# Sparse attention and gated FFN on one core: the last 128 rows of output in two column parts, 384 and 128

## The chip, the cores and the metric

One core of a Trainium2 chip runs the whole program. The metric is the device time in microseconds (us); the runs shown of the kernel before have a median of 295.41 us (five runs, 294.80 to 295.67). Apart from these, one execution was taken with the hardware profiler; all views below come from it.

## The reference

```python
# q, k, v: [4, 8, 768, 64] float32; chunk = 32, top_k = 6
ub   = sum(max(q * k_min[chunk], q * k_max[chunk]))      # bound of each query for each chunk of 32 keys
sel  = the 6 chunks of highest ub, causal chunks only
attn = softmax(where(sel & causal, q @ k.T / 8, -1e9))
x    = (attn @ v) as rows of 8 heads * 64                # [3072, 512]
gate = sigmoid(x @ w_gate); val = x @ w_val              # [3072, 1536]
out  = (gate * val) @ w_out                              # [3072, 512] float32
```

## The kernel before, in words

The 3072 rows of tokens are worked off in eight units `u0` to `u7` of 384 rows, that is three blocks of 128. For each unit there is an attention part (choice of chunks, scores, exponentials, values) and then `ffn(u, ...)` (L1131), the gated FFN of its 384 rows. The attention of a unit is woven into the FFN of the unit before it; the FFN of `u7` stands at the end with nothing beside it.

In `ffn`, twelve steps `fb` each multiply the transposed rows `xT_u` by a slice of 128 columns of `w_gate` into `g_u` and of `w_val` into `v_u` (four matmuls of 384 columns each, L1146). ScalarE (ACT) takes the tanh of `g_u` (L1154), VectorE (DVE) makes `hg_u` = (tanh + 1) * `v_u` (L1158). After that comes the output product, L1162 to L1181, three times, once for each block `tb` of 128 rows: three planned operations `o0`, `o1`, `o2` of four matmuls each add twelve products of `hg_u` (as the weights that are loaded into the array, 128x128) and `wo16` (512 columns) into one PSUM bank `o_u` (L1168); ACT or DVE scales it by 0.5 into the SBUF buffer `osb` (L1177, L1178); SyncE (SP) issues one DMA that stores 128 rows of 512 floats, 2048 bytes a row, to `out` (L1180).

```python
for tb in range(3):
    o = ps(f"o_{u.name}_{tb}", "ff", [128, 512])
...
    plan.add(f"out_{u.name}_{tb}", {SP: (350, 350)}, lambda e, r=r, osb=osb: nc.sync.dma_start(
        out[r:r + 128, :], at(osb)), reads=[osb], writes=[], prio=next_(EV) - 50, dma=(690, 2048))
```

The order of the work is planned before anything is emitted. Every operation is entered with `plan.add`: the engines that may do it with a cost for each, what it reads and writes, a priority. `Plan.walk` (L110) then places one operation after another on the engine on which it can start first, with PSUM banks (eight, of which category "ff" may hold four) and SBUF slots (two for `osb`) given out as they come free. Priorities are moved by a table of nudges (L304), and each DMA has an entry in a table of landing times, `LANDS`, by name. What comes out is one list, and each engine gets its instructions in the order of that list. The stores of outputs and the loads of q, k and v are issued by SP on one DMA queue; the weights are loaded by GpSimd (POOL). After its last store SP waits, one semaphore after the other, until all DMAs have landed, and then the engines meet at a barrier that ends the program (L1303).

Of the kernel before, what the change touches and what calls it, by code (L numbers as in the profile page):

```python
# [10 lines left out]
AF = mybir.ActivationFunctionType  # L11
# [5 lines left out]
PE, ACT, DVE, POOL, SP = "PE", "ACT", "DVE", "POOL", "SP"  # L17
# [486 lines left out]
q10_3:136270 q11_3:139900 v_2_5:126790 v_3_0:140810 v_3_1:141960 v_3_2:143110 out_u5_0:226380 out_u5_1:229010  # L504
out_u5_2:232390 v_3_3:144260 v_3_4:145410 v_3_5:146560 out_u6_0:260540 out_u6_1:263290 out_u6_2:266500
out_u7_0:284690 out_u7_1:287280 out_u7_2:290410
"""


def act(n, psum=True, parts=128):  # L510
    took = (170 if psum else 195) + n / 1.2
    return (took - 105 if parts == 128 else took + 10, took)


def dve(n, rate=1, parts=128):
    took = 158 + n / 0.96 / rate
    return (took - 80 if parts == 128 else took + 10, took)
# [7 lines left out]
def pe(busy, lag=170):  # L525
    return {PE: (busy, busy + lag)}
# [3 lines left out]
def kernel(  # L530
# [10 lines left out]
    nc = tc.nc  # L541
# [9 lines left out]
    NFB = D_FF // 128  # L551
    scale = 1.0 / (D ** 0.5)
# [5 lines left out]
    plan = Plan(  # L558
# [3 lines left out]
    )  # L562

    def at(b):
        if b.tile is None:
            b.tile = (banks if b.kind == "ps" else rot).tile(b.shape, b.dtype, tag=f"{b.kind}{b.slot}", name=b.name)
        return b.tile

    def ps(name, cat, shape, dtype=F32):
        return Buf("ps", name, shape, dtype, cat)  # L570
# [9 lines left out]
    def lone(name, shape, dtype=F16):  # L580
        return keep.tile(shape, dtype, tag=name, name=name)
# [10 lines left out]
    wo16 = lone("wo16", [128, NFB, 512])  # L592
# [6 lines left out]
    class Unit:  # L599
# [59 lines left out]
    units = [  # L659
        Unit(0, [], [(0, 0), (1, 1), (2, 2)]),  # L660
        Unit(1, [(0, 1), (0, 2), (0, 3)]),
        Unit(2, [(0, 4), (0, 5)], [(3, 2)]),
        Unit(3, [(1, 1), (1, 2), (1, 3)]),
        Unit(4, [(1, 4), (1, 5), (2, 1)]),
        Unit(5, [(2, 2), (2, 3), (2, 4)]),
        Unit(6, [(2, 5), (3, 1), (3, 2)]),
        Unit(7, [(3, 3), (3, 4), (3, 5)]),
    ]

    def rank(base, span, count):  # L670

        n = [0]

        def next_(ahead=0.0):
            n[0] += 1
            return base + span * min(1.0, (n[0] - 1) / count) - ahead

        return next_
# [12 lines left out]
    for i in range(2):  # L691
        const(f"kcr{i}", {DVE: (270, 280)}, lambda e, i=i: nc.vector.memset(kcr[i], 0.0),
              writes=[("kcr", i, jb, p, m) for jb in range(NBLK) for p in range(NP) for m in range(2)], prio=-8 if i == 0 else -1)
    for e_ in range(2):
        const(f"hq{e_}", {DVE: (150, 160)}, lambda e, e_=e_: nc.vector.memset(hq[1][e_][MASK[e_], :, 0:64], 0.0),
              writes=[("hqm", 1, e_, p, "zero") for p in range(NP)])
    for i in range(2):
        const(f"ap{i}", {DVE: (400, 410)}, lambda e, i=i: nc.vector.memset(ap[i], 0.0),
              writes=[("ap", i, 0), ("ap", i, 1)], prio=-0.5 + i)
        const(f"v1{i}", {POOL: (260, 300)}, lambda e, i=i: nc.gpsimd.memset(v16[i][:, :, :, D:D + 1], 1.0),  # L700
              writes=[("v16", i, jb) for jb in range(NBLK)], prio=-9 + 6 * i)
        for e_ in range(2):
            for o in range(2):
# [3 lines left out]
                      reads=[epat], writes=[("hkp", i, e_, p) for p in range(o, NP, 2)], prio=0.3 + 0.2 * i, port=True)  # L707
    const("ident16", {DVE: (150, 230)}, lambda e: nc.vector.tensor_copy(ident16, ident32),
          reads=["ident32"], writes=["ident16"], prio=-1.0)
# [421 lines left out]
    def ffn(u, base, span):  # L1131
        next_ = rank(base, span, NFB * 4 + 3 * 5)
        EV = 0.1
        hgs = []
        xt = [(u.xt, c) for c in range(4) if u.m] + [(u.xt, c, x) for c in range(4) for _, x in u.first]
        for fb in range(NFB):
            g = ps(f"g_{u.name}_{fb}", "ff", [128, T])
            w_ = ps(f"v_{u.name}_{fb}", "ff", [128, T])
            gate = Buf("gate", f"gate_{u.name}_{fb}", [128, T], F16)
            hg = Buf("hg", f"hg_{u.name}_{fb}", [128, T], F16)  # L1140
            hgs.append(hg)

            def product(t, w16, fb=fb):
                def emit(e):
                    for c in range(4):
                        nc.tensor.matmul(at(t), w16[:, c, 128 * fb:128 * fb + 128], at(u.xt)[:, c, :],  # L1146
                                         start=(c == 0), stop=(c == 3))
                return emit

            op = plan.add(f"g_{u.name}_{fb}", pe(650), product(g, wg16), reads=xt + [("wg", fb // 4)], writes=[g, "ffn"],  # L1150
                          prio=next_())
            plan.hold(op, gate)
            plan.hold(op, hg)
            plan.add(f"tanh_{u.name}_{fb}", {ACT: act(T)}, lambda e, g=g, gate=gate: nc.scalar.activation(  # L1154
                at(gate), at(g), AF.Tanh, scale=0.5), reads=[g], writes=[gate], prio=next_(EV))
            plan.add(f"v_{u.name}_{fb}", pe(650), product(w_, wv16), reads=xt + [("wv", fb // 4)], writes=[w_, "ffn"],
                     prio=next_())
            plan.add(f"hg_{u.name}_{fb}", {DVE: dve(T)}, lambda e, w_=w_, gate=gate, hg=hg: nc.vector.scalar_tensor_tensor(  # L1158
                at(hg), at(gate), 1.0, at(w_), ALU.add, ALU.mult), reads=[gate, w_], writes=[hg], prio=next_(EV))
        rows = {x: S * b + 128 * ib for x, (b, ib) in enumerate(u.blocks)}  # L1160
        rows.update({x: S * b for b, x in u.first})
        for tb in range(3):  # L1162
            o = ps(f"o_{u.name}_{tb}", "ff", [128, 512])
            osb = Buf("osb", f"osb_{u.name}_{tb}", [128, 512])
            for j in range(3):
                def project(e, o=o, tb=tb, j=j):
                    for fc in range(4 * j, 4 * j + 4):
                        nc.tensor.matmul(at(o), at(hgs[fc])[:, 128 * tb:128 * tb + 128], wo16[:, fc, :],  # L1168
                                         start=(fc == 0), stop=(fc == NFB - 1))

                op = plan.add(f"o{j}_{u.name}_{tb}", pe(4 * 215.6), project,
                              reads=hgs[4 * j:4 * j + 4] + [("wo", j)], writes=[o, "ffn"],
                              prio=next_())
                if j == 0:
                    plan.hold(op, osb)
            plan.add(f"osb_{u.name}_{tb}", {ACT: act(512), DVE: dve(512)}, lambda e, o=o, osb=osb: (
                nc.scalar.activation(at(osb), at(o), AF.Copy, scale=0.5) if e == ACT  # L1177
                else nc.vector.tensor_scalar_mul(at(osb), at(o), 0.5)), reads=[o], writes=[osb], prio=next_(EV))  # L1178
            r = rows[tb]
            plan.add(f"out_{u.name}_{tb}", {SP: (350, 350)}, lambda e, r=r, osb=osb: nc.sync.dma_start(  # L1180
                out[r:r + 128, :], at(osb)), reads=[osb], writes=[], prio=next_(EV) - 50, dma=(690, 2048))  # L1181


    for u in units:
# [25 lines left out]
    for ib in range(1, 4):  # L1210
        cast_v(0, ib, 0.5)
    ffn(units[0], 1.0, 0.95)

    load_wide(units[2], 0.1)
# [4 lines left out]
    for ib in range(4, 6):  # L1219
        cast_v(0, ib, 1.5)  # L1220
    attend(units[1], 1.0)
    ffn(units[1], 2.0, 0.95)

    def values_of(b, blocks, load, base):
# [11 lines left out]
    attend(units[2], 2.0)  # L1236
    first(units[2], 3, 2, raw_f[3], 2.0)
    ffn(units[2], 3.0, 0.95)

    values_of(1, range(4, 6), 2.1, 3.2)  # L1240
# [67 lines left out]
```

The softmax here doesn't subtract the row's maximum and nothing guards it: scores larger than these inputs give would overflow.

## Time and profile before

| what | before |
|---|---|
| median of the five runs shown | 295.41 us |
| the profiled execution's own time | 295.41 us |
| its span in the profile | 293.7 us |
| mean granted TensorE clock | 0.988 |
| PE busy (matmuls) | 277.6 us, 95% |
| ACT busy | 195.5 us, 67% |
| DVE busy | 188.5 us, 64% |
| stores of output, L1180 | 24 of 256 KB |
| start of the last block's scaling on ACT, L1177 | 289.88 us |
| issue of the last store on SP, L1180 | 290.50 us |
| end of the span | 293.7 us |

Times within the profile count from the span's start. The execution's own time is longer than the span by 1.7 us, which lie outside of what the profile shows. PE is TensorE's matmuls, PEld its weight loads, which lie beside matmuls; SPq is the queue of SyncE, which issues DMAs. In a chain of waits each line is a piece of the work that ended last: its start, its length, engine, tile and line.

### The profile page before, as it was taken

What the parts mean: (1) busy time and instruction counts of PE and PEld (TensorE: products, weight loads), DVE (VectorE), ACT (ScalarE), POOL (GpSimd) and SP (SyncE); (2) the same over time, 40 slices, a digit from 0 to 9 for tenths busy, and PEclk for the clock granted to TensorE, in tenths of its full rate; (3) what the DMA queues carried; (4) which work ended last, traced back from release to release, by engine and by line L of the source; (5) the groups of instructions that cost most, each with busy time, mean ns of one, the idle gap of its engine ahead of it and who ended that gap; (6) DMA issues with size and microseconds to landing.
All of it is one profiled execution on the core that took longest, in us unless ns stands there. A gap on an engine that the chain in (4) does not pass through costs nothing.

```text
span 293.7 us, 6954 instructions
## 1 busy us (share of the span) xinstructions
PE 277.6 (95%) x2656; PEld 176.3 (60%) x2656; DVE 188.5 (64%) x560; ACT 195.5 (67%) x398; POOL 91.6 (31%) x162
## 2 busy tenths in 40 slices
PE   2769998999989999999999999999999999999994
PEld 1544655767664666556666667676565556655651
DVE  8285883996999289999899899654134124432420
ACT  7674747977984879558889898886563467323321
POOL 5672314933652336013426854213000011000000
PEclk9977999999999999999999999999999999999999
DMA  7999999999977999299996300001100110011002
GB/s 158 219 250 217 197 197 241 220 146 165 150 135 93 203 187 204 47 215 161 140 218 134 105 3 3 0 2 39 71 2 1 54 56 0 2 38 71 0 16 93
DMA packets 123234, 32.69 MB, mean 111 GB/s; under 512 B 111425, under 2 KB 120129, under 8 KB 123201
## 3 DMA queue, kind: packets, MB, share of 16 engines
q1 hardware_dynamic: 118448, 27.53, 52.3%
q0 software_dynamic: 4752, 4.72, 9.5%
q8 instruction: 21, 0.34, 0.6%
q14 instruction: 13, 0.10, 0.1%
HBM read 30.67 MB, written 6.29 MB: 126 GB/s over the span
## 4 chain that ended last, share of the span: by engine, by line
PE 73%; DMA 12%; DVE 7%; SPq 3%; POOL 2%; issue 1%; ACT 0%; DVEq 0%; ACTq 0%
PE o_u L1168 20%; PE g_u L1146 16%; PE v_u L1146 16%; PE sc_u L1063 10%; DMA wo<-in_moe_w_out_dram 9%; PE pv_u L1096 6%; SPq L742 2%; PE ube_u L1002 2%; DMA kq_u<-in_k_dram 2%; DMA k<-in_k_dram 2%; PE xps_u L1123 2%; DVE kcr L787 1%; DVE kt L953 1%; DVE kx L787 1%; DVE qf_u L969 1%
## 5 line engine op out<-in xcount | busy, mean ns | idle before, releaser
L1074 ACT ACTIVATE att_u<-sc_u 128x512 f16<-128x512 f32 (+3 forms) x184 | 88.1, 550 | 14.3 <-PE sc_u L1063 13.4
L1158 DVE SCALAR_TENSOR_TENSOR hg_u<-gate_u,v_u 128x384 f16<-128x384 f16 x96 | 51.8, 544 | 54.1 <-PE v_u L1146 38.5
L1146 PE MATMUL g_u<-xT_u,wg 128*128 128x384 f16 x384 | 79.1, 329 | 0.0
L1146 PE MATMUL v_u<-xT_u,wv 128*128 128x384 f16 x384 | 78.7, 328 | 0.4 <-DMA wv<-in_moe_w_val_dram 0.4
L1154 ACT ACTIVATE gate_u<-g_u 128x384 f16<-128x384 f32 x96 | 47.6, 496 | 39.1 <-DVE hg_u L1158 21.5
L1168 PE MATMUL o_u<-wo,hg_u 128*128 128x512 f16 x288 | 68.1, 379 | 0.9 <-DMA wo<-in_moe_w_out_dram 0.9
L1080 POOL TENSOR_SCALAR_AFFINE_SELECT att_u<-att_u 128x384 f16<-128x384 f16 (+1 forms) x56 | 28.0, 506 | 101.2 <-ACT att_u L1074 100.4
L1146 PEld LDWEIGHTS <-wv 128*128 128x128 f16 x384 | 36.6, 98 | 23.5 <-DMA wv<-in_moe_w_val_dram 1.1
L1146 PEld LDWEIGHTS <-wg 128*128 128x128 f16 x384 | 36.5, 99 | 21.7 <-issue 1.5
L1168 PEld LDWEIGHTS <-hg_u 128*128 128x128 f16 x288 | 27.1, 98 | 28.5 <-issue 1.4
L1177 ACT ACTIVATE osb_u<-o_u 128x512 f32<-128x512 f32 x20 | 12.1, 603 | 26.7 <-PE o_u L1168 25.0
L1096 PEld LDWEIGHTS <-att_u 128*128 128x128 f16 x640 | 25.5, 98 | 4.7
L1096 PE MATMUL pv_u<-v,att_u 128*128 128x65 f16 x640 | 27.9, 193 | 0.0
L1063 PE MATMUL sc_u<-hqo,hko 128*128 128x128 f16 (+2 forms) x220 | 27.8, 243 | 0.1
L1063 PE MATMUL sc_u<-hqe,hke 128*128 128x128 f16 (+2 forms) x220 | 27.1, 243 | 0.2 <-ACT att_u L1074 0.2
L1063 PEld LDWEIGHTS <-hke 128*128 128x128 f16 x220 | 16.8, 98 | 5.7 <-issue 1.2
L779 POOL CAST v<-v 128x512 f16<-128x512 f32 x23 | 13.9, 617 | 17.4 <-DMA v<-in_v_dram 17.2
L1063 PEld LDWEIGHTS <-hko 128*128 128x128 f16 x220 | 16.3, 98 | 4.8 <-issue 0.2
L576 DVE COPY xT_u<-xps_u 128x384 f16<-128x384 f16 (+1 forms) x17 | 5.7, 338 | 14.4 <-PE xps_u L1123 14.3
L1115 DVE TENSOR_TENSOR x_u<-pv_u,rz_u 128x384 f16<-128x384 f32 (+1 forms) x28 | 14.5, 524 | 0.4
L1025 DVE MAX8 mx_u<-ubn_u 128x8 f32<-128x8 f32 (+16 forms) x152 | 12.4, 157 | 0.1
L787 DVE TRANSPOSE_TENSOR_REDUCE kcr<-k 128x24 f32<-128x768 f32 x12 | 11.2, 943 | 0.7 <-DMA k<-in_k_dram 0.7
(119 smaller groups left out, 305.1 us busy)
## 6 DMA issues: line engine op xcount, KB each, us to landing
out_dram<-osb_u SPq DMA_DIRECT2D x24, 256.0 KB, 2.5
v<-in_v_dram SPq DMA_DIRECT2D x23, 256.0 KB, 4.9
k<-in_k_dram SPq DMA_DIRECT2D x12, 384.0 KB, 5.9
q<-in_q_dram SPq DMA_DIRECT2D x12, 384.0 KB, 6.3
wg<-in_moe_w_gate_dram POOLq DMA_DIRECT2D x3, 512.0 KB, 9.5
wv<-in_moe_w_val_dram POOLq DMA_DIRECT2D x3, 512.0 KB, 11.9
wo<-in_moe_w_out_dram POOLq DMA_DIRECT2D x3, 512.0 KB, 22.4
kf<-in_k_dram SPq DMA_DIRECT2D x8, 128.0 KB, 3.9
```

The lines of the kernel that those rows point to most:

```text
L779: plan.add(f"v16_{b}_{ib}", {POOL: pool(H * D)}, lambda e: nc.gpsimd.tensor_copy(v16[b % 2][:, ib, :, 0:D], at(t)), reads=[t], writes=[("v ...
L787: plan.add(f"kx{m}_{name}_{p}", {DVE: dve(size)}, lambda e, m=m, op=op: nc.vector.tensor_reduce(out=outs[m](), in_=src(), op=op, axis=AX.X ...
L1025: nc.vector.max(at(mx)[:, e_, j, :], at(ubn)[:, e_, j, 0:max(8, u.seen[j])])
L1063: nc.tensor.matmul(at(t)[:, o:o + 128 * m], hk[b % 2][e_][:, p, 128 * jb:128 * jb + 128], hq[u.side][e_][:, p, 128 * x:128 * (x + m)], sta ...
L1074: plan.add(f"exp_{u.name}_{h}_{y}", {ACT: act(n)}, lambda e, t=t, att=att, b0=b0, n=n: nc.scalar.activation(at(att)[:, b0:b0 + n], at(t), ...
L1080: nc.gpsimd.affine_select(out=dv, in_=dv, compare_op=ALU.is_ge, fill=0.0, base=0, pattern=[[0, u.m], [1, 128]], channel_multiplier=-1)
L1096: nc.tensor.matmul(at(pv)[:, last, x, :], at(att)[:, c:c + 128], v16[b % 2][:, jb, h, :], start=(jb == 0), stop=(jb == ib))
L1115: plan.add(f"x_{u.name}_{p}", {DVE: dve(u.t)}, lambda e: nc.vector.tensor_tensor(at(x_).rearrange("p a (e d) -> p e a d", e=2), at(pv)[:, ...
L1146: nc.tensor.matmul(at(t), w16[:, c, 128 * fb:128 * fb + 128], at(u.xt)[:, c, :], start=(c == 0), stop=(c == 3))
L1154: plan.add(f"tanh_{u.name}_{fb}", {ACT: act(T)}, lambda e, g=g, gate=gate: nc.scalar.activation(at(gate), at(g), AF.Tanh, scale=0.5), read ...
L1158: plan.add(f"hg_{u.name}_{fb}", {DVE: dve(T)}, lambda e, w_=w_, gate=gate, hg=hg: nc.vector.scalar_tensor_tensor(at(hg), at(gate), 1.0, at ...
L1168: nc.tensor.matmul(at(o), at(hgs[fc])[:, 128 * tb:128 * tb + 128], wo16[:, fc, :], start=(fc == 0), stop=(fc == NFB - 1))
```

## The change

For the third block of `u7` alone, the last 128 rows that the program stores, the loop body of the output product runs twice: once for columns 0 to 383 and once for columns 384 to 511. Each part has its own PSUM buffer, its own twelve matmuls, its own scaling into its columns of the same `osb` buffer, and its own store. The weights `hg_u` are loaded once more for the second part. The table of landing times gets an entry for the added store.

```diff
+outb_u7_2:290410
...
         for tb in range(3):
-            o = ps(f"o_{u.name}_{tb}", "ff", [128, 512])
             osb = Buf("osb", f"osb_{u.name}_{tb}", [128, 512])
-            for j in range(3):
-                def project(e, o=o, tb=tb, j=j):
-                    for fc in range(4 * j, 4 * j + 4):
-                        nc.tensor.matmul(at(o), at(hgs[fc])[:, 128 * tb:128 * tb + 128], wo16[:, fc, :],
-                                         start=(fc == 0), stop=(fc == NFB - 1))
...
             r = rows[tb]
-            plan.add(f"out_{u.name}_{tb}", {SP: (350, 350)}, lambda e, r=r, osb=osb: nc.sync.dma_start(
-                out[r:r + 128, :], at(osb)), reads=[osb], writes=[], prio=next_(EV) - 50, dma=(690, 2048))
+            final = u is units[7] and tb == 2
+            for part, (lo, hi) in {"": (0, 384), "b": (384, 512)}.items() if final else [("", (0, 512))]:
+                o = ps(f"o{part}_{u.name}_{tb}", "ff", [128, hi - lo])
+                for j in range(3):
+                    def project(e, o=o, tb=tb, j=j, lo=lo, hi=hi):
+                        for fc in range(4 * j, 4 * j + 4):
+                            nc.tensor.matmul(at(o), at(hgs[fc])[:, 128 * tb:128 * tb + 128], wo16[:, fc, lo:hi],
+                                             start=(fc == 0), stop=(fc == NFB - 1))
+
+                    op = plan.add(f"o{j}{part}_{u.name}_{tb}", pe(4 * ((hi - lo) / 2.4 + 2.3)), project,
+                                  reads=hgs[4 * j:4 * j + 4] + [("wo", j)], writes=[o, "ffn"],
+                                  prio=next_())
+                    if j == 0 and not part:
+                        plan.hold(op, osb)
+                plan.add(f"osb{part}_{u.name}_{tb}", {ACT: act(hi - lo), DVE: dve(hi - lo)}, lambda e, o=o, osb=osb, lo=lo, hi=hi: (
+                    nc.scalar.activation(at(osb)[:, lo:hi], at(o), AF.Copy, scale=0.5) if e == ACT
+                    else nc.vector.tensor_scalar_mul(at(osb)[:, lo:hi], at(o), 0.5)), reads=[o], writes=[(osb, part)], prio=next_(EV))
+                plan.add(f"out{part}_{u.name}_{tb}", {SP: (350, 350)}, lambda e, r=r, osb=osb, lo=lo, hi=hi: nc.sync.dma_start(
+                    out[r:r + 128, lo:hi], at(osb)[:, lo:hi]), reads=[(osb, part)], writes=[], prio=next_(EV) - 50,
+                    dma=((hi - lo) * 1.35, 2048 if hi - lo > 128 else 512))
```

In the order that the plan gives, the two kernels are the same instruction for instruction on every engine up to this block. In the block, PE has 12 matmuls of 384 columns and then 12 of 128 (each with its weight load) where it had 12 of 512; ACT scales 128x384 and then 128x128 where it scaled 128x512; SP issues a store of 128 rows of 1536 bytes and then one of 128 rows of 512 bytes where it issued one of 128 rows of 2048 bytes. DVE and POOL have the same instructions as before.

More of the change, by code (lines that the diff above doesn't have):

```diff
@@ L1162, in ffn @@
         for tb in range(3):
-            o = ps(f"o_{u.name}_{tb}", "ff", [128, 512])
             osb = Buf("osb", f"osb_{u.name}_{tb}", [128, 512])
-            for j in range(3):
-                def project(e, o=o, tb=tb, j=j):
-                    for fc in range(4 * j, 4 * j + 4):
-                        nc.tensor.matmul(at(o), at(hgs[fc])[:, 128 * tb:128 * tb + 128], wo16[:, fc, :],
-                                         start=(fc == 0), stop=(fc == NFB - 1))
[L1171 to L1175, printed above, removed]
@@ L1176, in ffn @@
-            plan.add(f"osb_{u.name}_{tb}", {ACT: act(512), DVE: dve(512)}, lambda e, o=o, osb=osb: (
-                nc.scalar.activation(at(osb), at(o), AF.Copy, scale=0.5) if e == ACT
-                else nc.vector.tensor_scalar_mul(at(osb), at(o), 0.5)), reads=[o], writes=[osb], prio=next_(EV))
-            r = rows[tb]
-            plan.add(f"out_{u.name}_{tb}", {SP: (350, 350)}, lambda e, r=r, osb=osb: nc.sync.dma_start(
-                out[r:r + 128, :], at(osb)), reads=[osb], writes=[], prio=next_(EV) - 50, dma=(690, 2048))
+            r = rows[tb]
```

## The prediction

> **What bounds the kernel now.** The page's chain of work gives PE 73% of the span, but the change touches only what comes after the last FFN step. I therefore read the end of the run first, by the chain of waits from 284 us on. A line has start, length, engine, tile and line:
>
> ```profile
> 283.96 5.84 PE o_u L1168 x27
> 289.81 0.03 ACTq L1177
> 289.83 0.04 issue
> 289.88 0.60 ACT osb_u L1177
> ```
>
> PE runs its 36 output matmuls without a gap: 5.84 us / 27 = 0.2163 us each. ACT starts 0.07 us after the last and ends at 290.48. Next is the timeline of SP alone, then the DMA view from 290 to 294 us. Its 40 slices are 0.1 us each:
>
> ```profile
> 290.50 0.33 SPq L1180 DMA_DIRECT2D out_dram<-osb_u  x1
> DMA  0000000000000599999930000000000000000000
> GB/s 0 0 0 0 0 0 0 0 0 0 0 0 0 205 369 451 389 348 389 348 123 0 0 0 0 0 0 0 0 0 0 0 0 0 0 0 0 0 0 0
> out_dram<-osb_u SPq DMA_DIRECT2D x1, 256.0 KB, 2.0
> ```
>
> The reader is to see that the last store is alone. It is issued at 290.50, its bytes begin to move 0.83 us later (in the fourteenth slice; a window of 291.2 to 292.3 puts it at 291.33), move for 0.75 us (to 292.08), and land 2.0 us after the issue, at 292.5. What follows is SP's, seen in its waits from 289 us on and in its semaphore instructions from 292.45 to 292.88:
>
> ```profile
> SPq L1303 <- DMA out_dram<-osb_u: 1.5, 1, 1.5
> L1303 SPq EVENT_SEMAPHORE  x6: 28/28/28, 292.5 to 292.8; - x6
> ```
>
> SP waits for that landing, then steps over six semaphores, 292.5 to 292.8, 0.06 us each, and the closing barrier runs to 293.7. So **the tail after PE** sets the end: eviction 0.60, start of the store 0.83, bytes 0.75, landing 0.4, closing 1.2. The change can only win there, and only a few tenths.
>
> **The change part by part.**
>
> *Order.* Up to this block both kernels issue the same instructions in the same order on every engine, and the inputs of the block's matmuls are long there (DVE's last hg_u ends at 282.7). Nothing before 287.2 us moves. The eviction of the first part waits for the osb slot of the store issued at 285.27, which lands at 287.3, two us before it is needed.
>
> *PE.* Twelve matmuls of 512 columns go: 12 x 0.2163 = 2.595 us. Twelve of 384 come, and twelve of 128, each with its weight load. The chain has the pace of both, with the weight load beside them:
>
> ```profile
> 270.32 0.65 PE g_u L1146 x4
> 235.51 0.17 PE xps_u L1123 x3
> ```
>
> 0.65 / 4 = 0.1625 and 0.17 / 3 = 0.057: 12 x 0.1625 + 12 x 0.057 = 1.95 + 0.68 = 2.63 us. **+0.035 us**, all on the path. The granted clock is 1.00 from 275 us to the end, so the pace holds. The added weight loads have a row here (98 ns each, loaded beside the matmul before), so the two ends are 0 and 0.1 us; I take the row's pace.
>
> The Trainium skill speaks against this: "TensorE: Matmul & The Clock Gate", section "Back-to-back issue gap", gives about 81 ns as the sustained spacing of weight load and matmul at 128 columns. By it the twelve would take 0.97 us and the PE term would be about +0.33, an estimate from that page. The trace's xps_u has just such pairs at 57 ns, so the measurement decides.
>
> *Eviction.* The last one shrinks from 128x512 to 128x128. There is no 128x128 of L1177, but ACT's other PSUM reads show every size:
>
> ```profile
> L1177 ACT ACTIVATE osb_u<-o_u 128x512 f32<-128x512 f32 x20 | 12.1, 603 | 26.7 <-PE o_u L1168 25.0 <-issue 1.5
> L1074 ACT ACTIVATE att_u<-sc_u 128x512 f16<-128x512 f32 x120 | 66.6, 604 | 12.8 <-PE sc_u L1063 12.3
> L1074 ACT ACTIVATE att_u<-sc_u 128x384 f16<-128x384 f32 x40 | 19.0, 500 | 1.1 <-PE sc_u L1063 1.1
> L1074 ACT ACTIVATE att_u<-sc_u 128x128 f16<-128x128 f32 x8 | 2.1, 280 | 0.1
> ```
>
> At 512 columns the two lines agree (603 and 604 ns), so I take 280 ns for 128; the last three evictions took 597 each. **-0.32 us.** The first part's eviction (0.50) is hidden under the second part's matmuls: its PE work ends at 289.80 - 2.595 + 1.95 = 289.155, ACT runs 289.23 to 289.73, and the second part's starts at 289.91. If that cover were gone it would cost up to 0.5. Behind the second eviction nothing is queued on ACT.
>
> *Issue on SP.* The first store is issued at 289.75. SP took 0.33 for the last store; where a load follows a store (49.84, then 50.30; 123.92, then 124.38) the next issue starts 0.46 after. So SP is free for the second at 290.21, and its data are ready at 290.48 + 0.035 - 0.32 = 290.19; the second issue is at 290.22. That is a tie; a slower SP would cost a few hundredths. Against 290.50 the last issue is 0.28 earlier. Behind it SP has only the closing waits.
>
> *Bytes.* The first store moves 3/4 of the bytes: from 290.58 for 0.75 x 0.75 = 0.56 us, to 291.14. The second may start at 290.22 + 0.83 = 291.05, and queues 0.09 behind it. A store with rows of 512 bytes isn't in this trace. From below, a quarter of the bytes is 0.19 us (0.15 at the fastest slice above, 451 GB/s). Loads in 512-byte packets (the DMA view of 47.9 to 48.7 us) ran at
>
> ```profile
> DMA packets 469, 0.22 MB, mean 280 GB/s; under 512 B 32, under 2 KB 469, under 8 KB 469
> ```
>
> which makes 0.23 us for 64 KB. From above, 128 small packets could cost as much as the 128 big ones of before: 0.75 us. I take 0.23, since the packet size is the same. The bytes are then out at 291.14 + 0.23 = 291.37 instead of 292.08: -0.71, of which -0.28 is the earlier issue counted above and **-0.43** is the shorter transfer. That the second store starts without a gap rests on 123.92: the load issued behind that store moves on in the next slices with no idle slice between, long before the store has landed.
>
> The skill's "DMA: Bandwidth & Descriptors", section "Measured (HBM→SBUF, 128 partitions, SWDGE, issued from GpSimd)", gives 0.95 us for 64 KB and asks to batch; by its figure the second store would be out at about 292.1 and nothing would be won in the transfer (an estimate). Here 256 KB took 0.75, less than that figure for a quarter of the bytes, on another queue, so I don't use it.
>
> *Closing.* The added store signals the semaphore that SP checks next, so five checks are left after the last landing instead of six: **-0.06 us**. Bounds: 0 and -0.06.
>
> Sum: +0.035 - 0.32 - 0.43 - 0.06 = -0.77 us (0.035 - 0.32 is the 0.28 above). The profiled execution's own time is 295.41, 1.7 us over its span, and equals the median of the runs shown, so the sum is made against 295.41: **294.65 us**, -0.26%. What this kernel's measurement can tell from no change is about 0.2%, 0.59 us.
>
> Bounds: all gains at their best (0.15 for the second store's bytes, no queueing behind the first) give -0.9, 294.5. With every packet of both stores at the cost of a 2 KB one, the first is out at 291.33, the second at 292.08: only the closing's 0.06 is left, 295.35.
>
> **The rivals.**
>
> 1. *Small packets cost as big ones.* A DMA engine may need a fixed time for each packet it writes, whatever its size. For it: nothing in the trace shows a 512-byte write. Against it: 512-byte loads ran at 280 GB/s. If the second store's packets alone cost that, it is out at 291.14 + 0.75 = 291.89: -0.19 - 0.06 = -0.25, **295.15 us**. Within 0.2%.
>
> 2. *The second store is held until the first has landed* (slower). For it: SP's issues took 3.52 us at 56.05 and 2.76 us at 126.66, so an issue can be held. The first store lands at 289.75 + 2.0 - 0.19 = 291.56; a second issued then lands 2.0 - 0.52 = 1.48 us later, at 293.04, against 292.5: +0.54 - 0.06 = +0.48, **295.9 us**. It turns the sign from the point where the second issue is held more than 0.77 us beyond 290.22. Against it: those two issues stood behind loads of small packets, the queue here has 128 packets ahead, and at 49.84 and 123.92 the next issue followed within 0.46 us.
>
> 3. *Nothing comes of it*: another engine's closing work ends last, **295.4 us**. Against it: SP's wait for this store is 1.5 us long, and its waits for all others from 289 us on come to 0.7, in the barrier after it.
>
> **How the numbers follow.** Forecast 0.70, rival 1 0.20, rival 2 0.07, rival 3 0.03. The forecast's gain lies only 0.18 us beyond the 0.59 us that counts as faster, and the five runs spread over 0.87, so a median can be off by 0.1 to 0.2: of its 0.70 I give 0.60 to faster and 0.10 to the same. Of rival 1, 0.04 to faster (if the cost lies between the ends), 0.14 same, 0.02 slower by scatter; rival 2 is slower with 0.07; rival 3 is the same. Together faster 0.64, same 0.27, slower 0.09. The range goes from the best bound less 0.1 of scatter, 294.4, to rival 1 with little scatter, 295.2; what is left out is the worst bound, rivals 2 and 3.
>
> **What would show it.** In the profile after: PE's last matmul some 0.03 us later; ACT's last L1177 at 289.91 with 280 ns; two SPq issues at 289.75 and 290.22; the DMA view busy without a gap from 290.6 to 291.4; SP's first closing check near 291.8 with five left. It would be wrong if the 512-byte packets took far more than 29 ns each (512 bytes at 280 GB/s / 16 engines), if the second issue came late, or if a gap stood between the two stores' bytes.

## The result and the profile after

| | before | changed |
|---|---|---|
| median | 295.71 us (78 runs, 294.39 to 297.61) | 294.91 us (41 runs, 293.90 to 296.23) |
| ratio, 95% interval | | 0.9968, 0.9958 to 0.9978 |
| the profiled execution's own time | 295.41 us | 294.98 us |
| its span | 293.7 us | 293.3 us |
| tail: start of the eviction of the block before the last, to the end of the span | 6.47 us (287.24 to 293.71) | 5.80 us (287.48 to 293.28) |

The change is faster by 0.32%, 0.65 to 1.24 us by the interval (the medians differ by 0.80). Forecast was -0.77 us. A single execution spreads over some 3 us, so the readings below rest on the tail, which the profile gives to a hundredth. It is counted from a mark that both kernels have, the start of ACT's eviction of the block before the last; an eviction is the scaling that takes a finished product out of PSUM into `osb`. In the timelines of ACT, before and changed:

```profile
287.24 0.60 ACT L1177 ACTIVATE osb_u<-o_u 128x512 f32<-128x512 f32 x1 [1.99 <-PE o_u L1168]
287.48 0.60 ACT L1181 ACTIVATE osb_u<-o_u 128x512 f32<-128x512 f32 x1 [1.99 <-PE o_u L1172]
```

In the changed kernel's profiled execution the mark is 0.24 us later than in before's, though all work ahead of it is the same; counted from the mark, the tail is 0.67 us shorter.

The chain of waits of the changed kernel, from 284 us on:

```profile
283.99 5.40 PE o_u L1172 x28
289.39 0.68 PE ob_u L1172 x12
290.08 0.02 issue
290.10 0.28 ACT osb_u L1181
```

PE works without a gap to the end and the twelve matmuls of 128 columns take 0.68 us, 0.057 each. The last eviction has shrunk from 0.60 to 0.28. The timeline of ACT shows the two parts (start, length, line, tiles, form, idle time before):

```profile
289.48 0.49 ACT L1181 ACTIVATE osb_u<-o_u 128x384 f32<-128x384 f32 x1 [1.40 <-PE o_u L1172]
290.10 0.28 ACT L1181 ACTIVATE osb_u<-ob_u 128x128 f32<-128x128 f32 x1
```

The first part is evicted while PE multiplies the second, and is done 0.13 us before the second's eviction starts. The DMA view from 290 to 294 us, in slices of 0.1 us, and SP's waits from 289 us on:

```profile
DMA  0000000059999899300000000000000000000000
GB/s 0 0 0 0 0 0 0 0 215 338 384 338 415 292 287 261 93 0 0 0 0 0 0 0 0 0 0 0 0 0 0 0 0 0 0 0 0 0 0 0
...
out_dram<-osb_u SPq DMA_DIRECT2D x1, 192.0 KB, 1.9
out_dram<-osb_u SPq DMA_DIRECT2D x1, 64.0 KB, 1.7
```

```profile
SPq L1307 <- DMA out_dram<-osb_u: 1.1, 2, 0.9
```

Two stores, one busy stretch: the bytes move from 290.83 to 291.71 without an idle slice, at 338 to 415 GB/s while they are the first store's and at 261 to 292 when the second's follow. SP's one wait of 1.5 us for a landing has become two, 0.9 us for the first store and 0.2 for the second.

### The profile page after: what moved, and what is told of

The parts are those of the page before. It is cut to its first block, busy times and chain, and to the rows that moved or that the text cites. A ratio compares the mean times of both kernels' runs of the same rounds, so it can differ in the third digit from the quotient of the medians.

```text
span 293.3 us, 6981 instructions
## 1 busy us (share of the span) xinstructions
PE 277.9 (95%) x2668; PEld 177.2 (60%) x2668; DVE 188.5 (64%) x560; ACT 195.6 (67%) x399; POOL 91.8 (31%) x162
## 4 chain that ended last, share of the span: by engine, by line
PE 73%; DMA 13%; DVE 7%; SPq 3%; POOL 2%; issue 1%; ACT 0%; DVEq 0%; ACTq 0%
PE o_u L1172 20%; PE g_u L1147 16%; PE v_u L1147 16%; PE sc_u L1064 10%; DMA wo<-in_moe_w_out_dram 9%; PE pv_u L1097 6%; SPq L743 2%; DMA kq_u<-in_k_dram 2%; PE ube_u L1003 2%; DMA k<-in_k_dram 2%; PE xps_u L1124 2%; DVE kcr L788 1%; DVE kt L954 1%; DVE kx L788 1%; DVE qf_u L970 1%
## 5 line engine op out<-in xcount | busy, mean ns | idle before, releaser
L1172 PE MATMUL o_u<-wo,hg_u 128*128 128x512 f16 (+1 forms) x288 | 67.4, 377 | 0.9 <-DMA wo<-in_moe_w_out_dram 0.9
L1172 PEld LDWEIGHTS <-hg_u 128*128 128x128 f16 x300 | 27.9, 98 | 28.1 <-issue 1.4
L1181 ACT ACTIVATE osb_u<-o_u 128x512 f32<-128x512 f32 (+1 forms) x20 | 12.0, 598 | 26.1 <-PE o_u L1172 24.4
```

## The experiments

The measure is the tail as in the table. It takes in the last block's matmuls, evictions, stores and the closing, and nothing before; its start is an ACT line of the timeline that all these kernels share.

| kernel | tail, us | against before | expected by the theory | ratio of times (95%) |
|---|---|---|---|---|
| before | 6.47 | | | |
| changed | 5.80 | -0.67 | | 0.9968 (0.9958 to 0.9978) |
| the changed kernel again (e0) | 5.81 | -0.66 | 5.80 | 0.9971 (0.9952 to 0.9989) |
| two parts, one store (e1) | 6.13 | -0.33 | 6.18 | 0.9994 (0.9973 to 1.0015) |
| one part, two stores (e2) | 6.55 | +0.08 | 6.41 to 6.55 | 1.0017 (0.9996 to 1.0038) |
| 128, then 384 (e3) | 6.18 | -0.29 | 6.14 to 6.22 | one execution |
| 256 and 256 (e4) | 5.91 | -0.55 | 5.86 to 5.93 | one execution |
| 320 and 192 (e5) | 5.78 | -0.69 | 5.71 to 5.78 | 0.9984 (0.9967 to 1.0002) |
| before, last semaphore last (r5) | 6.18 | -0.29 | 6.17 | 0.9996 (0.9975 to 1.0017) |
| changed, last semaphore last (r4) | 5.52 | -0.95 | 5.56 | 0.9956 (0.9937 to 0.9974) |
| 256, 128, 128 (t3) | 5.61 | -0.86 | 5.61 to 5.68 | 0.9966 (0.9947 to 0.9985) |
| 256, 128, 128, last semaphore last (t3 and r3) | 5.43 | -1.04 | 5.43 | 0.9970 (0.9951 to 0.9988) |

**Theory.** After PE's last matmul nothing is left but a chain: last eviction, issue, 0.83 us until bytes move, bytes, landing, SP's closing checks. Splitting shortens the last eviction, and lets all but the last store's bytes move early. **Rivals.** The eviction is all of the gain, or the smaller last store is all of it, or part of the time comes from earlier in the program.

### One half of the change at a time: e1 and e2

e1 keeps the two products and evictions of the changed kernel but stores the block by one DMA:

```diff
+                if final and not part:
+                    continue
+                lo_, keys = (0, [(osb, ""), (osb, "b")]) if final else (lo, [(osb, part)])
-                    out[r:r + 128, lo:hi], at(osb)[:, lo:hi]), reads=[(osb, part)], ...
+                    out[r:r + 128, lo:hi], at(osb)[:, lo:hi]), reads=keys, ...
```

> The last block is multiplied and scaled in the parts 384 and 128, but stored by one DMA of 256 KB after the second eviction. Measure: the tail, from the start of the eviction of the block before to the end of the span: 6.47 us before (287.24 to 293.71), 5.80 with the change (287.48 to 293.28). My theory is that the shorter eviction and the shorter last transfer are each worth about half: the eviction alone gives -0.28, the transfer keeps its 0.82, six closing checks: tail 6.18. Rival: the eviction is all of the gain, because the bytes of the first store lie before those of the second anyway: tail 5.80. Rival: the smaller last store is all of it, the eviction being hidden by the issue of the first store: tail 6.47.

The chip gave 6.13. e1's DMA view from 290 to 294 us and its last eviction:

```profile
289.95 0.28 ACT L1181 ACTIVATE osb_u<-ob_u 128x128 f32<-128x128 f32 x1
```

```profile
DMA  0000000000289999961000000000000000000000
GB/s 0 0 0 0 0 0 0 0 0 0 82 328 369 389 348 430 389 246 41 0 0 0 0 0 0 0 0 0 0 0 0 0 0 0 0 0 0 0 0 0
...
out_dram<-osb_u SPq DMA_DIRECT2D x1, 256.0 KB, 2.0
```

The eviction is the short one, but 256 KB move after it and land 2.0 us after the issue, as before. So the shorter eviction alone is worth 0.33, half of the change. Both rivals of "all" fall: 5.80 and 6.47 were theirs.

e2 keeps one product and one eviction and cuts only the store:

```diff
+            cuts = [(0, 384), (384, 512)] if u is units[7] and tb == 2 else [(0, 512)]
-                out[r:r + 128, :], at(osb)), ...
+                out[r:r + 128, lo:hi], at(osb)[:, lo:hi]) for lo, hi in cuts], ...
```

> The last block is multiplied and scaled whole, as before, and stored by two DMAs of 384 and 128 columns, issued one after the other. My theory: the second issue comes 0.43 after the first, its bytes queue behind the first's, and end at about the time of the one store before; closing one check less: tail 6.41 to 6.55 us against 6.47. Rival, a small last store is worth something by itself: tail below 6.2. Rival, a second store costs a second full start: tail above 6.9.

It gave 6.55, 0.08 more than before. Its DMA view from 290 to 294 us:

```profile
DMA  0000000000000002999898950000000000000000
...
out_dram<-osb_u SPq DMA_DIRECT2D x1, 192.0 KB, 1.9
out_dram<-osb_u SPq DMA_DIRECT2D x1, 64.0 KB, 1.8
```

The two stores move in one stretch of about 0.9 us (291.56 to 292.45) where one store took 0.8. A small last store is worth nothing if all data are ready at once. The halves don't add: -0.33 and +0.08 apart, -0.67 together, because the first store can only move early once its part is multiplied and evicted early.

### Where to cut: e3, e4, e5

```diff
-            for part, (lo, hi) in {"": (0, 384), "b": (384, 512)}.items() if final else ...
+            for part, (lo, hi) in {"": (0, 128), "b": (128, 512)}.items() if final else ...   # e3
+            for part, (lo, hi) in {"": (0, 256), "b": (256, 512)}.items() if final else ...   # e4
+            for part, (lo, hi) in {"": (0, 320), "b": (320, 512)}.items() if final else ...   # e5
```

> The same split with the parts exchanged: 128 columns first, 384 last. My theory: last eviction 0.49 instead of 0.28, last bytes 0.69 of which none is hidden behind an earlier store: the bytes end 0.26 earlier than before, tail 6.14 to 6.22 us. Rival, eviction is all: 0.49 + 0.035 against 0.60, tail 6.40. Rival, that a split of any kind is worth the same: 5.80.

> The same split in 256 and 256 columns. My theory: last eviction 0.39, the first store is out long before, the last bytes (8 packets of 1 KB on each DMA engine) take 0.49: tail 5.86 to 5.93 us, a little more than the 5.80 of the change. Rival, that the landing after small packets is what keeps the change from more: with 1 KB rows the time from last byte to SP's check would go back from 0.43 to 0.36.

> The split at 320 and 192 columns. In the changed kernel the second store's bytes (from 291.35) follow at once on the first's, 0.1 later than its issue alone would have let them. If the first store's bytes are what sets the end there, they come 0.35 earlier with 320 columns, and the second store (192 columns, eviction 0.34, bytes 0.40) ends by its own path: tail 5.71 to 5.78 us. Rival, the second part's own path is the bound already: it grows by 0.06 of eviction and 0.05 of bytes, tail 5.90.

6.18, 5.91 and 5.78. The last evictions were 0.49, 0.38 and 0.33 us for 384, 256 and 192 columns, and the tail follows the size of the last part as the theory has it, down to 192. From there to 128 nothing is gained (5.78 and 5.80): the rival of e5, that the last part's own path is the bound already, would have 5.90. e5's DMA view from 290 to 294 us has idle slices between the two stores, which the changed kernel's has not:

```profile
DMA  0000049998300189820000000000000000000000
```

The trace's packets show what comes in: in e5 the second store's bytes start 0.83 us after its issue, on idle DMA engines; in the changed kernel 0.93 us after it, at 291.35, which is when a DMA engine is through with its eight packets of the first store (290.83 + 8 x 0.065). This 0.10, with 0.02 at the issue and 0.03 at the landing, uses up what the smaller part gains in eviction (0.06) and bytes (0.07). e4's question on landing has its answer in the last section.

### The closing: r5 and r4

Five (r5) or four (r4) earlier stores, which lie beside matmuls, are cut in two, so that the last store's semaphore is the last that SP checks:

```diff
+            cuts = [(0, 256), (256, 512)] if f"{u.name}_{tb}" in ['u5_0', 'u5_1', 'u5_2', 'u6_0', 'u6_1'] else [(0, 512)]
-                out[r:r + 128, :], at(osb)), ...
+                out[r:r + 128, lo:hi], at(osb)[:, lo:hi]) for lo, hi in cuts], ...
```

> The kernel before, with five earlier stores (three of the sixth unit, two of the seventh) each cut in two column halves, so that the last store signals the last of the semaphores that SP checks: one check after the landing instead of six. Those earlier stores lie beside matmuls. My theory of the closing: 0.06 us for each check, tail 6.47 - 0.30 = 6.17 us, time -0.1%. Rival: the checks are not on the path (the barrier waits for something else): tail 6.47.

> The changed kernel, with four earlier stores cut in two, so that the last store signals the last semaphore that SP checks. My theory: tail 5.80 - 0.24 = 5.56 us, and the rest of the tail as in the changed kernel (second issue 0.43 after the first, landing 0.43 after the last bytes). Rival: no change of the tail, 5.80.

(In r4 the stores are `u5_1`, `u5_2`, `u6_0` and `u6_1`.) The tails are 6.18 against 6.47, and 5.52 against 5.80. SP's waits in r5 from 289 us on, and its semaphore instructions between 292 and 293 us:

```profile
SPq L1305 <- DMA out_dram<-osb_u: 1.2, 1, 1.2
```

```profile
L1305 SPq DRAIN  x3: 7/7/7, 292.5 to 292.8; - x3
L1305 SPq EVENT_SEMAPHORE  x2: 17/22/28, 292.4 to 292.7; - x2
```

The wait is 1.2 us where it was 1.5, and after the landing SP goes on at once to the barrier (DRAIN); the five checks that stood there are now done while the landing is awaited. So a check after the landing is 0.06 us on the path, as the prediction's closing term had it. The times alone could not show it for r5 (0.9996, 0.9975 to 1.0017); 0.29 us is 0.1%.

### Three parts, and all together: t3, t3 and r3

```diff
+... outc_u7_2:290410
...
-            for part, (lo, hi) in {"": (0, 384), "b": (384, 512)}.items() if final else ...
+            for part, (lo, hi) in {"": (0, 256), "b": (256, 384), "c": (384, 512)}.items() if final else ...
```

> Three parts, 256, 128 and 128 columns. My theory: the first two stores are out before the last one's bytes begin, the last part's path is eviction 0.28 and bytes 0.35; two closing checks less than before; PE 0.06 more than before: tail 5.61 to 5.68 us. Rival: SP's issues, 0.43 apart, or the third eviction behind the second become the bound: tail 5.8 or more.

> The two things that shortened the tail most, together: three parts (256, 128, 128) and three earlier stores cut in two so that the last store signals the last of the semaphores that SP checks. My theory, adding the pieces: tail 5.61 - 0.18 = 5.43 us, 1.04 less than before, time -0.35%. Rival: the pieces are not independent, the checks are gone through while the landing is awaited anyway: tail 5.61.

The tail is 5.61, and with three earlier stores cut as in r4 (`u5_2`, `u6_0`, `u6_1`) 5.43. ACT's timeline in t3 and r3 together:

```profile
288.21 0.39 ACT L1181 ACTIVATE osb_u<-o_u 128x256 f32<-128x256 f32 x1 [0.76 <-PE o_u L1172]
288.83 0.28 ACT L1181 ACTIVATE osb_u<-ob_u 128x128 f32<-128x128 f32 x1 [0.24 <-PE ob_u L1172]
289.50 0.28 ACT L1181 ACTIVATE osb_u<-oc_u 128x128 f32<-128x128 f32 x1 [0.39 <-PE oc_u L1172]
```

ACT is idle before each part, and waits for PE each time, so the third eviction is no bound, nor are SP's issues (0.51 and 0.67 apart). Of the 0.19 that t3 gains over the changed kernel, 0.14 lie between the last issue and its check, since the last store's bytes start 0.83 us after the issue and not 0.93; one check less is 0.06, and PE's added work takes 0.03 back. The two together, t3 and r3, have the shortest tail, 1.04 us less than before. Their time (0.9970) can't be told from the changed kernel's.

### Did time come from elsewhere? e0

The interval of the changed kernel reaches to 1.24 us, and its middle, 0.95, is more than the tail's 0.67. e0 is the changed kernel unaltered.

> The changed kernel once more, unaltered, for the scatter. My theory: the tail repeats within 0.03 us (5.80, second store's landing check 0.43 after its last bytes), while the start of the last block moves by several tenths between executions, which is why the times spread far more than the tail explains. Rival: the time gained beyond the tail is real and comes from earlier in the program: the last block then starts earlier here than before's 287.04 us.

The tail was 5.81, with the second store's check 0.44 after its last bytes. The mark was at 287.17 us, 0.07 earlier than before's 287.24, where the first profile of the change had it 0.24 later, at 287.48. Over all twelve profiles it lies between 286.85 (t3 and r3) and 288.46 us (t3), which have the same work before it but for stores that are cut beside matmuls. So the start of the last block moves by 1.6 us from execution to execution, and no gain ahead of it is seen.

The other kernels bear on this too. For all nine that have a ratio in the table, the difference of the tail lies within the interval of the times. The gain by the ratio is between 0.42 us less and 0.35 us more than the gain of the tail, and on the mean of the nine the two agree (0.02 us apart). That the rest of 0.95 is scatter fits this, but is not shown: the changed kernel, e0 and r4, which share the last block, all gain more by the ratio than by the tail (0.28, 0.20 and 0.35).

## Why the prediction was right

The forecast was -0.77 us by the sum of four terms; the tail shows -0.67. The medians' -0.80 is no better proof of the forecast, since the interval of the times reaches from 0.65 to 1.24. Term by term, each time counted from the first matmul of the last block in its own execution:

| step | predicted | measured |
|---|---|---|
| first matmul to last eviction | +0.035 | -0.02 (2.84 to 2.82) |
| last eviction | -0.32 | -0.32 (0.597 to 0.277) |
| eviction's end to issue | 0.00 | +0.02 (0.025 to 0.044) |
| issue to last byte | -0.43 | -0.36 (1.66 to 1.30) |
| last byte to SP's check | 0 | +0.07 (0.36 to 0.43) |
| check to the end | -0.06 | -0.06 (1.19 to 1.13) |
| sum | -0.77 | -0.67 |

- **PE.** The pace of 0.1625 and 0.057 us held, and PE was 0.03 us later as forecast. What was not foreseen: ACT started 0.036 us after the last matmul's modelled end, where it started 0.086 after it in before (the prediction read 0.07, and kept it). The chain of before has a piece "ACTq" of 0.03 ahead of its eviction, which the chain after does not have; the last eviction after waits for PE alone, that of before also for the landing of an earlier store and for ACT's own work. The same holds in the other runs: 0.036 to 0.038 in all whose last eviction waits for PE alone, 0.086 in e2 and r5, which have before's. That the number of waits makes the difference fits, but wasn't tried by itself. The 81 ns of the Trainium skill's "TensorE: Matmul & The Clock Gate", section "Back-to-back issue gap", did not show: here the twelve took 0.68 us, 57 ns each with their weight loads.
- **Eviction.** 277 ns against 280 from the 128x128 row of another ACT instruction that reads PSUM.
- **Issue.** SP's issues stand 0.425 apart, and the tie that the prediction spoke of cost 0.02: from the eviction's end to the issue it is 0.042 to 0.044 us in the changed kernel, e0 and r4, and 0.026 in e1, e3, e4, e5 and t3, where SP has long been free.
- **Bytes.** This is the term of the sum that was mis-sized: "I take 0.23". The packets of 512 bytes were as cheap as the loads said: the trace's records have 27 ns for one (65 ns for 1536 bytes, 86 for 2048). So rival 1, small packets at the price of big ones, is refuted by the packets themselves. But the stretch from the first packet to the last byte was 0.37 us for the second store, where eight packets of 27 ns, an engine's share, make 0.22. A like excess, 0.13, stood in before: 0.82 us from first to last (the prediction read 0.75), where eight of 86 ns are 0.69. Part of it is that the 16 DMA engines don't start together: the first sixteen packets of before's store start over 0.09 us. A sum by GB/s leaves it out. Both ends were put too early, the one after by 0.14 and the one before by 0.08, which leaves 0.07 in the term. The queueing of 0.09 behind the first store came true at 0.10.
- **Landing.** The sum left it as it was; 0.07 was missing, for a reason that stays open.
- **Rival 2**, a second store held until the first has landed: the second was issued 1.47 us before SP saw the first landed. Refuted. **Rival 3**, that nothing comes of it, is refuted by the tail.

The three terms that came out too small in gain (0.07, 0.07 and 0.02), less the 0.05 that PE and ACT gave back, make up the 0.10 between -0.77 and -0.67, but for rounding. So the mechanism held, and a part of the sum's closeness is errors that offset each other.

## What to carry to other kernels

When a kernel ends in matmul, eviction, store and landing, the last piece's size sets the tail: cut the last block so that the early part's eviction lies under the matmuls of the late part, and the early store's bytes move while the late part is evicted, issued and on its way to its first byte (0.83 us here). Make the last part smaller until the early store's bytes are just out of the way (here, in two parts, 192 and 128 columns were the same). Splitting the store without splitting the work ahead of it gains nothing (+0.08 us here), and splitting the work without the store gains half (-0.33). For changes of a few tenths of a microsecond, read a stretch of the profile that starts at a line which both kernels share: it repeated within 0.01 us here (5.80 and 5.81), where the time itself spread over 3 us.

## What the runs showed of the hardware

- SP checks the DMA semaphores one after another at the end, 0.06 us each. Each store that is added ahead of the last moves the last one's signal on by one semaphore: six checks from its landing on in before, five in the changed kernel, four in t3, one in r5. Moving it to the end of the list was worth 0.29 us in before (five checks) and 0.28 in the changed kernel (four checks; the landing was 0.05 shorter in that execution).
- The time from a store's last byte to SP's check was 0.35 to 0.37 us where it moved in packets of 2048 bytes (before, e1, r5), 0.39 to 0.40 at 1536, 1024 and 768 bytes (e3, e4, e5) and 0.38 to 0.44 at 512 (changed, e0, e2, r4, t3, t3 and r3). e4's rival, that it goes back from 0.43 to 0.36 with 1 KB rows, is not borne out: it was 0.40. Why it grows stays open.
- Packets of a store took 27, 36, 46, 55, 65 and 86 ns at 512, 768, 1024, 1280, 1536 and 2048 bytes: close to a line of 7 ns and 0.0385 ns a byte. In every kernel the last store's stretch from first packet to last byte was longer than its eight packets on an engine, by 0.13 to 0.16 us.
